# Attention, a gated network and a squared-clip network on one core: stores of the weight work, its allowances, and when k, v and streamed halves are asked for

## The chip, the cores and the metric

The kernel runs on 1 core of one Trainium2 chip. The metric is device time in microseconds (us), the median of several runs. Engines are written as in the profile: PE (TensorE, PEld its weight loads), DVE (VectorE), ACT (ScalarE), POOL (GpSimd) and SP (SyncE, which here issues all DMAs; SPq is its queue).

## What is computed

```python
kv = np.einsum('bhsd,bhse->bhde', k, v)              # 8 batches, 8 heads, 576 positions, 64
out = np.einsum('bhsd,bhde->bhse', q, kv)
rms = np.sqrt(np.mean(out * out, axis=-1, keepdims=True) + 1e-06)
x = (out / rms * g_norm)                             # then 4608 tokens x 512
x = (sigmoid(x @ w_gate) * (x @ w_val)) @ w_out      # 512 -> 1536 -> 512
h = x @ w_in                                         # 512 -> 2048
g = np.where(h >= 1, h, np.where(h <= -1, 0, (h + 1) ** 2 / 4))
return g @ w_out2                                    # 2048 -> 512
```

## The kernel before

Everything is float32. A product is made of three products of rounded halves (`mm3`, L86 to L90): high by high, high by low, low by high. `split` (L66) makes the two halves of an operand: ACT copies the high one (L69), DVE subtracts to get the low one (L77). The weights arrive as 64-bit words and are decoded on the chip.

The 4608 tokens are 9 blocks `j` of 512, and the 1536 hidden columns are 12 blocks `f`. Blocks 0 and 1 are done first, together. Blocks 2, 3 and 4 go one after the other, in 12 steps `f` each (loop from L1173): the sums for gate and value of `f + 1` (24 matmuls, `h`), sigmoid and product (`gf`, L553), the halves of that (`gh`, `gl`), then the 12 matmuls of `down(j, f)` into `acc`. Block 4 is called the tail. The attention and the normalisation of the next block run beside these steps (`norm_stage` in five stages, placed by `norm_plan` at points (f, 0), (f, 1), (f, 2)).

Blocks 5, 6 and 7, 8 are two pairs (`Pair`, loop from L1225). A pair computes gate and value of both blocks by seven products of half-size blocks (`pA` to `pE`, L631) in place of eight; it needs for that seven combinations of each weight block, which are read from DRAM (`w1d`). After the 12 steps of a pair come `down(j + 1, 0)`, `down(j, 11)`, and then the last down phase, `down(j + 1, f)` for f = 1 to 11, 12 matmuls each. The second network (`Second`) does the same trick with `w2d` and `wo2d`.

The weight work makes these combinations. It is one long list of single instructions (`weights_work`): for each `f` the stores of the halves of gate and value, two sums (`wsum`), four combinations (`su`), and their halves (`halves_out`, tiles `w2half`) with stores; then 24 units for the second network, each with a load (`raw`), a decode (one ACT, five DVE instructions, L463 to L473), combinations, halves and stores. Every entry is marked D (DVE), A (ACT) or S (a store). `work(dve, act)` (L1162) takes entries from the list until a kind is used up:

```python
left, begun = {"D": dve, "A": act, "S": 1}, False
while ahead[0] and left[ahead[0]] and not (begun and ahead[0] == "S"):
    left[ahead[0]] -= 1
    begun = True
    ahead[0] = next(todo, None)
```

so an S ends an allowance unless it comes first in it. Calls of `work` stand twice in each step of blocks 2 to 4 and three times in each step of a pair. What is left after the last pair's steps is done at once (`while ahead[0]: work(9, 9)`, L1274), ahead of `store(j)`, of the halves for the rest of the last down phase and of the x and weights of the second network (`second.begin()`).

All loads and stores stand in one order on SP. The halves of the down weights (`woh`) are streamed from DRAM by `stream_wo`; `stream(n)` asks for more until n are held.

Of the kernel before, what the change touches and what calls it, by code (L numbers as in the profile page):

```python
# [33 lines left out]
def attn_gated_mlp_kernel(ctx: ExitStack, tc: tile.TileContext, a: dict, out: bass.AP):  # L34
# [204 lines left out]
    def norm_plan(chunks, every):  # L239

        plan = {}
        for i, (j, p) in enumerate(chunks):
            f = every * i
            for n, place in enumerate(((f, 2), (f + 1, 0), (f + 1, 1), (f + 1, 2), (f + 2, 1))):
                plan.setdefault(place, []).append((j, p, n))
        for place in plan.values():
            place.sort(key=lambda x: -x[2])
        return plan
# [178 lines left out]
    OPS = ("a11", "a12", "a22", "s1", "s2", "s4", "s3")  # L427

    def w1_steps(f):

        gate, value = (wgv[f, i] for i in range(2))
        d = w1d[f]
        yield "S"
        store_halves(gate, [d[:, 0:2, h] for h in range(2)])
        store_halves([t[:, 2 * P:] for t in value], [d[:, 2, h] for h in range(2)])
        ts = []
# [54 lines left out]
    def halves_out(src, dst):  # L491

        n = src.shape[-1]
        halves = [half_tile(wop, "w2half", "wo")[:, :n] for _ in range(2)]
        yield "A"
        act_copy(halves[0], src)
        yield "D"
        nc.vector.tensor_tensor(out=halves[1], in0=src, in1=halves[0].bitcast(F32), op=ALU.subtract)
        yield "S"
        store_halves(halves, [dst(h) for h in range(2)])  # L500

# [81 lines left out]
    class Pair:  # L583
# [59 lines left out]
        def step(self, side, j, f, at, more):  # L643
# [13 lines left out]
            u2 = saved(A, "u2", "sig", 1)  # L657
            work(1, 1)
            D = bank(side, 2, "pD")
# [13 lines left out]
            at(3)  # L673
            work(2, 1)
            if f == F1 - 1:
# [259 lines left out]
    with tc.manual_schedule():  # L935
# [226 lines left out]
        def work(dve, act):  # L1162

            left, begun = {"D": dve, "A": act, "S": 1}, False
            while ahead[0] and left[ahead[0]] and not (begun and ahead[0] == "S"):
                left[ahead[0]] -= 1
                begun = True
                ahead[0] = next(todo, None)

        last = NB - 1  # L1170
        pair = Pair()
        chunks = lambda *js: [(j, p) for j in js for p in range(NP)]
        for j in range(2, J0):  # L1173
            tail = j == J0 - 1
# [6 lines left out]
            for f in range(F1):  # L1181
# [4 lines left out]
                if f + 1 < F1:  # L1186
                    g = gate_value(f + 1, xs)
                    split_g(j, f + 1, g)
                if not tail:
                    work(4, 2)  # L1190
                elif f < 9:
                    work(2, 1)
                at(f, 1)
                if j + 2 < B and f in ((2, 5) if tail else (3, 7)):
# [12 lines left out]
                if not tail:  # L1207
                    work(4, 2)
                elif f < 8:
# [8 lines left out]
                if tail and f == 9:  # L1218
                    pair.load(1)

        kv_done = J0 + 1
        pairs = range(J0, NB, 2)
# [6 lines left out]
        for k, j in enumerate(pairs):  # L1229
# [6 lines left out]
            if more:  # L1236
# [5 lines left out]
                for u in range(2):  # L1242
                    b = ((j + 3 + u) * T - 1) // S
                    if b > kv_done:
                        kv_done = b
                        for i in range(2):
                            plan.setdefault((4 * u + i, 2), []).insert(0, (kv_product, b, i))
                            for p in range(2 * i, 2 * i + 2):
                                plan.setdefault((4 * u + i - 1, 3), []).append((load_kv, b, p))
                        if u == 0:  # L1250
                            for p in range(2):
                                load_kv(b, p)

# [19 lines left out]
            else:  # L1273
                while ahead[0]:  # L1274
                    work(9, 9)
                store(j)
                early_end.close()
                second = Second()
                second.begin()
            for f in range(1, F1):  # L1280
                if f + 1 < F1:
                    split_g(j + 1, f + 1, pair.g2[f + 1])
                if more:
                    run(steps, 3)
                    if f in (3, 6):
                        pair.load(f // 3 - 1)
                else:
                    if f > 1:
# [52 lines left out]
```

## Time and profile before

| | us |
|---|---|
| median of 3 runs (1823.65 to 1828.53) | 1827.46 |
| the profiled execution | 1818.42 |
| its span | 1816.6 |
| PE busy (94%) | 1710.7 |
| DVE busy (60%) | 1081.4 |
| ACT busy (45%) | 816.1 |

The span of the trace lies within the profiled execution's own time. The share of busy time is an average over stages; where PE is idle, the list of its waits tells what ended each wait, and the tables by window tell what the other engines and the DMAs did in a stretch. PEclk is the granted clock of PE as a share of 2.4 GHz.

### The profile page before, as it was taken

To read this page: it belongs to the slowest core of one execution; us is meant where nothing else is said; L and a number is where in the kernel's file an instruction comes from. 1 tells how busy PE (TensorE), PEld (TensorE's weight loads), DVE (VectorE), ACT (ScalarE), POOL (GpSimd) and SP (SyncE) were. 2 spreads that over 40 slices of the span, in tenths; PEclk is the share of its full clock that TensorE was granted. 3 is DMA by queue.
4 is the path that set the end of the run, shared out by engine and by line. 5 is a ranking of instruction groups with operands and counts; after the bars stand their busy time and mean duration, and the time that the engine had idled before them with its cause. 6 is when DMAs were issued, how large, how long until landed. Compare 5 with 4: busy or idle time off the path is not lost.

```text
span 1816.6 us, 23149 instructions
## 1 busy us (share of the span) xinstructions
PE 1710.7 (94%) x8552; PEld 1444.6 (80%) x8552; DVE 1081.4 (60%) x1898; ACT 816.1 (45%) x1391; POOL 1.0 (0%) x8
## 2 busy tenths in 40 slices
PE   8999999999999899999990299999999999999999
PEld 5778787888877777788870189899899898998997
DVE  3788745464556567765666455655655556556553
ACT  3353445445376477643342244434444444444442
POOL 0000000000000000000000000000000000000000
PEclk7999999999999999999995599999999999999999
DMA  8554687566645767596755776344344343342430
GB/s 222 180 179 158 209 278 234 187 215 210 218 148 185 249 219 247 189 374 222 275 165 194 267 265 249 108 180 156 116 163 157 116 162 134 139 163 93 180 122 35
DMA packets 156832, 343.45 MB, mean 189 GB/s; under 512 B 15400, under 2 KB 64680, under 8 KB 150576
## 3 DMA queue, kind: packets, MB, share of 16 engines
q1 hardware_dynamic: 156720, 341.98, 55.5%
q8 instruction: 67, 1.10, 0.3%
q14 instruction: 45, 0.37, 0.1%
HBM read 264.85 MB, written 77.07 MB: 188 GB/s over the span
## 4 chain that ended last, share of the span: by engine, by line
PE 86%; DVE 7%; DMA 3%; ACT 2%; issue 1%; SPq 0%; DVEq 0%; ACTq 0%
PE acc L89 9%; PE acc L88 9%; PE acc L90 9%; PE h L88 6%; PE h L89 6%; PE h L90 6%; PE chB L775 6%; PE pA L631 5%; PE chA L775 4%; PE acc L775 4%; PE pE L631 3%; PE chC L775 3%; PE chD L775 3%; PE pC L631 2%; PE pD L631 2%; DMA raw<-in_w 1%
## 5 line engine op out<-in xcount | busy, mean ns | idle before, releaser
L88 PE MATMUL acc<-gh,woh 128*128 128x512 f32 x432 | 172.4, 399 | 80.7 <-ACT gh L69 71.1
L89 PE MATMUL acc<-gl,woh 128*128 128x512 f32 x432 | 171.2, 396 | 2.9 <-DVE gl L77 2.9
L88 PEld LDWEIGHTS acc<-gh,woh 128*128 128x128 f32 x432 | 82.1, 190 | 102.1 <-ACT gh L69 71.9
L88 PE MATMUL h<-xh,w 128*128 128x512 f32 x384 | 152.3, 397 | 0.0
L89 PE MATMUL h<-xl,w 128*128 128x512 f32 x384 | 150.4, 392 | 0.1
L90 PE MATMUL h<-xh,w 128*128 128x512 f32 x384 | 150.4, 392 | 0.0
L90 PE MATMUL acc<-gh,woh 128*128 128x512 f32 x336 | 132.7, 395 | 0.2 <-DMA woh<-wo1d 0.2
L90 PE MATMUL acc<-wo,gh 128*128 128x512 f32 x336 | 132.4, 394 | 0.0
L89 PE MATMUL acc<-wo,gh 128*128 128x512 f32 x336 | 132.2, 394 | 0.0
L88 PE MATMUL acc<-wo,gh 128*128 128x512 f32 x336 | 130.9, 390 | 0.0
L631 PE MATMUL pA<-xc,wc 128*128 128x512 f32 x432 | 110.8, 392 | 0.5 <-ACT s L69 0.5
L553 DVE TENSOR_TENSOR gf<-sig,h 128x512 f32<-128x512 f32 x60 | 41.2, 687 | 100.5 <-PE h L90 87.9
L89 PEld LDWEIGHTS acc<-gl,woh 128*128 128x128 f32 x432 | 82.2, 190 | 22.3 <-DVE gl L77 4.8
L69 ACT ACTIVATE gh<-g 128x384 fp32r<-128x384 f32 (+1 forms) x120 | 63.5, 541 | 76.4 <-PE acc L90 54.6
L631 PEld LDWEIGHTS pA<-xc,wc 128*128 128x128 f32 x432 | 81.3, 189 | 18.2 <-ACT s L69 1.0
L88 PEld LDWEIGHTS h<-xh,w 128*128 128x128 f32 x384 | 72.7, 189 | 20.1 <-issue 4.4
L704 DVE TENSOR_TENSOR gh<-c,gh 128x384 fp32r<-128x384 f32 x96 | 53.6, 558 | 57.3 <-ACT gh L69 56.6
L89 PEld LDWEIGHTS h<-xl,w 128*128 128x128 f32 x384 | 72.7, 189 | 15.1 <-DVE xl L77 0.4
L90 PEld LDWEIGHTS h<-xh,w 128*128 128x128 f32 x384 | 72.5, 189 | 15.2
L704 DVE TENSOR_TENSOR c<-chD,p 128x384 f32<-128x384 f32 x48 | 26.8, 558 | 92.1 <-ACT v L787 81.4
L90 PEld LDWEIGHTS acc<-gh,woh 128*128 128x128 f32 x336 | 64.2, 191 | 14.2 <-DMA woh<-wo1d 0.6
L704 DVE TENSOR_TENSOR g<-vp,g 128x768 f32<-128x768 f32 x48 | 46.0, 959 | 48.2 <-ACT vp L787 48.2
(222 smaller groups left out, 3807.0 us busy)
## 6 DMA issues: line engine op xcount, KB each, us to landing
wst<-w2d SPq DMA_DIRECT2D x48, 1792.0 KB, 7.4
woh<-wo1d SPq DMA_DIRECT2D x168, 256.0 KB, 5.0
wc<-w1d SPq DMA_DIRECT2D x168, 256.0 KB, 5.3
raw<-in_w SPq DMA_DIRECT2D x32, 512.0 KB, 4.9
raw<-in_w_gv SPq DMA_DIRECT2D x24, 512.0 KB, 4.3
w1d<-w2half SPq DMA_DIRECT2D x48, 256.0 KB, 2.2
w2d<-w2half SPq DMA_DIRECT2D x48, 256.0 KB, 2.8
kvraw<-in_kv_main SPq DMA_DIRECT2D x24, 448.0 KB, 5.3
```

What stands on the lines that cost most here:

```text
L69: nc.scalar.activation(out=o, in_=i, func=AF.Copy)
L88: nc.tensor.matmul(ps, w[0][:, wsl], x[0], start=first, stop=False)
L89: nc.tensor.matmul(ps, w[0][:, wsl], x[1], start=False, stop=False)
L90: nc.tensor.matmul(ps, w[1][:, wsl], x[0], start=False, stop=last)
L553: nc.vector.tensor_tensor(out=g, in0=sig, in1=value, op=ALU.mult)
L631: nc.tensor.matmul(o, w[:, h, sl], x[c][l], start=first and c == n == 0, stop=c == 1 and n == 2, skip_group_check=True)
L704: nc.vector.tensor_tensor(out=o, in0=x, in1=y, op=op)
L775: nc.tensor.matmul(bank[:, :T2], self.ws[w][h][:, sl], self.xo[x][:, l, c], start=first and c == n == 0, stop=c == 1 and n == 2, skip_grou ...
```

## The change

Stores of the weight work are put in a list `stores` and written out at the start of the next `work` call; they are no entries of the work list any more, so nothing but D and A ends an allowance. Allowances change: `work(5, 2)` for `work(4, 2)` at the end of a step of blocks 2 and 3; in a step of a pair `(1, 1), (1, 1), (3, 0)` in the first and `(2, 1), (3, 1), (3, 0)` in the second, for `(1, 1), (2, 1), (3, 0)` in both. In blocks 2 to 4 the norm stage at point 1 stands before the halves of `gf` and the weight work, not behind them, and `norm_plan` sorts the stages of a point the other way (stage 0 last). The k and v that the first pair needs are asked for in step 9 of the tail (`kv_ahead`), not at the pair's start. After the last pair's `store(j)`, `stream(6)` asks for halves before `second.begin()`.

```diff
@@ norm_plan
-            place.sort(key=lambda x: -x[2])
+            place.sort(key=lambda x: x[2] if x[2] else 9)
@@ w1_steps, halves_out
+    stores = []
...
-        yield "S"
-        store_halves(gate, [d[:, 0:2, h] for h in range(2)])
-        store_halves([t[:, 2 * P:] for t in value], [d[:, 2, h] for h in range(2)])
+        stores.append((gate, [d[:, 0:2, h] for h in range(2)]))
+        stores.append(([t[:, 2 * P:] for t in value], [d[:, 2, h] for h in range(2)]))
...
-        yield "S"
-        store_halves(halves, [dst(h) for h in range(2)])
+        stores.append((halves, [dst(h) for h in range(2)]))
@@ Pair.step
-            work(1, 1)
+            work(1, 1) if more else work(2, 1)
...
-            work(2, 1)
+            work(1, 1) if more else work(3, 1)
@@ work
-            left, begun = {"D": dve, "A": act, "S": 1}, False
-            while ahead[0] and left[ahead[0]] and not (begun and ahead[0] == "S"):
+            while stores:
+                store_halves(*stores.pop(0))
+            left = {"D": dve, "A": act}
+            while ahead[0] and left[ahead[0]]:
                 left[ahead[0]] -= 1
-                begun = True
                 ahead[0] = next(todo, None)
@@
+        kv_done = [J0 + 1]
+
+        def kv_ahead(j):
+
+            b = ((j + 3) * T - 1) // S
+            if j + 2 < NB and b > kv_done[0]:
+                for p in range(2):
+                    load_kv(b, p)
@@ blocks 2 to 4
                 if f + 1 < F1:
                     g = gate_value(f + 1, xs)
+                at(f, 1)
+                if f + 1 < F1:
                     split_g(j, f + 1, g)
                 if not tail:
                     work(4, 2)
                 elif f < 9:
                     work(2, 1)
-                at(f, 1)
...
                 if not tail:
-                    work(4, 2)
+                    work(5, 2)
...
                 if tail and f == 9:
                     pair.load(1)
+                    kv_ahead(J0)
@@ pairs
-                        if u == 0:
-                            for p in range(2):
-                                load_kv(b, p)
...
-                while ahead[0]:
+                while ahead[0] or stores:
                     work(9, 9)
                 store(j)
+                stream(6)
                 early_end.close()
                 second = Second()
                 second.begin()
...
+                    if f == 9:
+                        kv_ahead(j + 2)
```

What this moves is seen in the order of the instructions on three engines.

DVE in a step of block 2, before, from the product `gf` of one step to that of the next (`w2half`: a half of the weight work, `m` and `t`: the norm stages, `kvw`: a copy of a k v product):

```order
L553 TENSOR_TENSOR gf<-sig,h_2926 128x512
L77 TENSOR_TENSOR gl<-gf,gh 128x512
L498 TENSOR_TENSOR w2half<-su,w2half 128x512
L225 TENSOR_SCALAR m<-SS 128x512
L72 COPY kvw_187<-kvps 128x128
L230 TENSOR_TENSOR t<-t,m 128x512
L553 TENSOR_TENSOR gf<-sig,h_3020 128x512
```

and the like step of the changed kernel, to within a row of its next `gf`:

```order
L553 TENSOR_TENSOR gf<-sig,h_2963 128x512
L225 TENSOR_SCALAR m<-SS 128x512
L77 TENSOR_TENSOR gl<-gf,gh 128x512
L454 TENSOR_TENSOR su<-su,wsum 128x256
L454 TENSOR_TENSOR su<-wsum,su 128x256
L454 TENSOR_TENSOR su<-wsum 128x256
L499 TENSOR_TENSOR w2half<-su,w2half 128x512
L72 COPY kvw_187<-kvps 128x128
L230 TENSOR_TENSOR t<-t,m 128x512
L499 TENSOR_TENSOR w2half<-su,w2half 128x512
L441 TENSOR_TENSOR wsum<-w 128x512 x2
L454 TENSOR_TENSOR su<-wsum 128x256
```

One weight instruction stood there where eight and more stand now, and `m` has come ahead of `gl`.

ACT behind the last pair's steps, before (`raw`, `dt`: the decode; `ev`: the copies of `store(j)`; `gh<-g`: halves for the last down phase; `x_b<-xin`: the second network's x):

```order
L463 ACTIVATE dt<-raw 128x512
L69 ACTIVATE w2half<-dt 128x512
L463 ACTIVATE dt<-raw 128x512
L69 ACTIVATE w2half<-dt 128x512
L69 ACTIVATE ev<-acc_7732 128x512
L69 ACTIVATE ev<-acc_7734 128x512
L69 ACTIVATE gh<-g_7832 128x512
L69 ACTIVATE gh<-g_7937 128x512
L69 ACTIVATE x_b_9204<-xin 128x768
L69 ACTIVATE gh<-g_8046 128x512
```

and now, from the last product of the pair (`u<-pA`):

```order
L69 ACTIVATE u_9064<-pA 128x512
L69 ACTIVATE gh<-g_7920 128x512
L69 ACTIVATE gh<-u_9064 128x512
L69 ACTIVATE gh<-g_8014 128x512
L69 ACTIVATE ev<-acc_8023 128x512
L69 ACTIVATE ev<-acc_8025 128x512
L69 ACTIVATE gh<-g_8127 128x512
L69 ACTIVATE gh<-g_8236 128x512
L69 ACTIVATE x_b_9208<-xin 128x768
L69 ACTIVATE gh<-g_8348 128x512
```

No decode stands ahead of `ev` and `gh` any more; `x_b` still stands ahead of the halves of `down(j + 1, 4)`.

SP at the same place, before (`wo1d`: streamed halves in DRAM, `wst`: weights of the second network):

```order
L523 DMA wo2d_145<-w2half 128x512 x2
L580 DMA x2d_177<-ev 128x512 x4
L736 DMA xin<-x2d_170 128x2x256 x2
L736 DMA xin<-x2d_171 128x2x256
L736 DMA xin<-x2d_170 128x2x256 x2
L736 DMA xin<-x2d_171 128x2x256
L724 DMA wst<-w2d_98 128x3584
L529 DMA woh<-wo1d_0_112 128x512
```

and now:

```order
L580 DMA x2d_177<-ev 128x512 x4
L529 DMA woh<-wo1d_0_112 128x512
L529 DMA woh<-wo1d_1_113 128x512
L529 DMA woh<-wo1d_0_114 128x512
L529 DMA woh<-wo1d_1_115 128x512
L529 DMA woh<-wo1d_0_116 128x512
L529 DMA woh<-wo1d_1_117 128x512
L529 DMA woh<-wo1d_0_118 128x512
L529 DMA woh<-wo1d_1_119 128x512
L736 DMA xin<-x2d_170 128x2x256 x2
L736 DMA xin<-x2d_171 128x2x256
```

Eight loads of halves have come ahead of the loads of x and of the second network's weights.

## Rows read from the trace of the kernel before

**Rows 1.** The page, 40 equal slices of the span.

```profile
PE   8999999999999899999990299999999999999999
...
PEclk7999999999999999999995599999999999999999
```

**Rows 2.** Waits of PE, whole span: us in total, times, longest us.

```profile
PE acc L88 <- ACT gh L69: 71.1, 2, 70.1
PE acc L88 <- DMA woh<-wo1d: 9.6, 1, 9.6
```

**Rows 3.** Windows: us, then busy (x instructions) by engine, PEclk, DMA share, GB/s.

```profile
952.70:1022.80 70.10, 0.00 (x0) 0.00 (x0) 48.00 (x87) 18.61 (x33) 0.00 (x0) 0.54 0.57 190
1022.80:1043.40 20.60, 10.72 (x24) 7.60 (x25) 4.98 (x7) 2.68 (x4) 0.00 (x0) 0.59 1.00 361
```

**Rows 4.** Timeline of PE, last down phase: start us, us, instruction [idle before].

```profile
949.80 0.39 PE L88 MATMUL acc<-gh,woh 128*128 128x512 f32 x1
...
952.29 0.39 PE L90 MATMUL acc<-gh,woh 128*128 128x512 f32 x1
...
1022.81 0.79 PE L88 MATMUL acc<-gh,woh 128*128 128x512 f32 x1 [70.14 <-ACT gh L69]
...
1039.10 0.63 PE L89 MATMUL acc<-gl,woh 128*128 128x512 f32 x1
...
1042.51 0.63 PE L88 MATMUL acc<-gh,woh 128*128 128x512 f32 x1
...
1065.44 1.23 PE L775 MATMUL chA<-x_b,wst 128*128 128x384 f32 x6
```

**Rows 5.** Groups on DVE, 952.7 to 1022.8: xcount, busy us, mean ns, idle before.

```profile
L469 DVE SCALAR_TENSOR_TENSOR dt<-raw,dt 128x512 f32<-128x512 uint32 x11 | 7.6, 693 | 0.4
...
L498 DVE TENSOR_TENSOR w2half<-dt,w2half 128x512 fp32r<-128x512 f32 x9 | 6.2, 689 | 4.2 <-ACT w2half L69 4.2
...
L465 DVE TENSOR_SCALAR du<-dt 128x512 uint32<-128x512 uint32 x11 | 4.7, 424 | 17.5 <-ACT dt L463 17.5
```

**Rows 6.** Timeline of SP, last down phase.

```profile
1022.62 1.80 SPq L580 DMA_DIRECT2D x2d<-ev  x4
1024.52 3.47 SPq L736 DMA_DIRECT2D xin<-x2d  x6
1028.09 0.41 SPq L724 DMA_DIRECT2D wst<-w2d  x1
1028.60 15.74 SPq L529 DMA_DIRECT2D woh<-wo1d  x14
```

**Rows 7.** Timeline of ACT, last down phase.

```profile
1028.89 0.84 ACT L69 ACTIVATE x_b<-xin 128x768 fp32r<-128x768 f32 x1 [5.61 <-DMA xin<-x2d]
```

**Rows 8.** Windows, blocks 2 and 3.

```profile
267.80:371.80 104.00, 104.00 (x548) 84.59 (x547) 56.03 (x100) 48.06 (x74) 0.00 (x0) 1.00 0.64 204
371.80:477.30 105.50, 105.50 (x554) 85.85 (x553) 57.46 (x102) 48.29 (x75) 0.00 (x0) 1.00 0.67 212
```

**Rows 9.** Waits of DVE, 267.8 to 477.3 (blocks 2 and 3).

```profile
DVE gf L553 <- PE h L90: 66.0, 23, 5.5
DVE gl L77 <- ACT gh L69: 16.1, 23, 0.7
```

**Rows 10.** Waits of PE, 500 to 560 (block 4).

```profile
PE X L178 <- DVE m L225: 4.2, 3, 2.1
```

**Rows 11.** Waits of PE, 560 to 610 (into the first pair).

```profile
PE kvps L154 <- DMA kvraw<-in_kv_main: 3.9, 2, 2.1
```

**Rows 12.** Timeline of PE, first pair's first step.

```profile
600.52 1.52 PE L631 MATMUL pE<-xc,wc 128*128 128x512 f32 x6
604.15 0.33 PE L154 MATMUL kvps<-kvraw 112*64 112x64 f32 x2 [2.11 <-DMA kvraw<-in_kv_main]
...
608.46 2.27 PE L631 MATMUL pA<-xc,wc 128*128 128x512 f32 x6
```

**Rows 13.** DMA issues of the page: xcount, KB each, us to landing.

```profile
woh<-wo1d SPq DMA_DIRECT2D x168, 256.0 KB, 5.0
```

More of the change, by code (lines that the diff above doesn't have):

```diff
@@ L1219, in attn_gated_mlp_kernel @@
                     pair.load(1)
-        kv_done = J0 + 1
+                    kv_ahead(J0)
         pairs = range(J0, NB, 2)
@@ L1243, in attn_gated_mlp_kernel @@
                     b = ((j + 3 + u) * T - 1) // S
-                    if b > kv_done:
-                        kv_done = b
+                    if b > kv_done[0]:
+                        kv_done[0] = b
                         for i in range(2):
```

## The prediction

> **What bounds the kernel now.** I read the page's slices first. PE is busy nine tenths or more nearly everywhere, but two neighbouring slices past the middle show 0 and 2, with the granted clock at 5 tenths [rows 1]. Then the list of PE's waits, to see who ended them: one single wait of 70.1 us ended by ACT (`gh`), and one of 9.6 us ended by a load of streamed halves [rows 2]. The windows around them show what the others did: for 70.1 us PE does nothing while DVE is busy 48.0 us with 87 instructions, and in the 20.6 us after it PE has a mean clock of 0.59 and the DMAs a share of 1.00 at 361 GB/s [rows 3]. The groups on DVE in that stretch are the decode and the halves of the weight work [rows 5]. So the place is the drain of what the work list still holds after the last pair: `gh` for `down(j + 1, 2)` stands behind it on ACT. Everywhere else PE is the bound, with short waits before the first pair [rows 10, 11].
>
> The reader should see in the PE timeline how long the last down phase is [rows 4]: twelve matmuls of `down(j + 1, 1)` start from 949.80 to 952.29, 0.2264 us apart (2.49 over 11), so one `down` is 2.72 us. `down(j + 1, 2)` could start at 952.52; the second network starts at 1065.44. That is 112.9 us for ten downs worth 27.2 us, so **85.7 us** of this phase are not PE's work at full clock: 70.1 of drain, 9.6 of waiting for halves, and some 5 of slow matmuls (0.426 us apart from 1039.10 to 1042.51, eight intervals).
>
> **The change, part by part.**
>
> *The drain.* The work list, counted against the allowances as the code has them, holds 336 D and 104 A. Before, 84 S stand between them, and the steps of blocks 2, 3, 4 and of the two pairs take 48, 52, 30, 55 and 60 D; 91 D and 31 A are left. Without S in the list they take 108, 101, 31, 52 and 44 D, and the list is empty in step 8 of the last pair. The order on ACT says the same: no decode stands ahead of `ev` and `gh` there. So the 85.7 us go, less what the last down phase will wait for instead.
>
> *What is late next there.* Call T the end of `down(j, 11)` (949.8). The four stores of `ev` follow one after the other and take 1.8 us to issue [rows 6], so SP is free for the eight loads of `stream(6)` at about T + 1.5. The halves of `down(j + 1, 3)` land 5.0 us later [rows 13], T + 6.5, and are wanted at T + 5.4: a wait of 1.1. Eight issues at 0.45 us, then x: issued from T + 5.1. Before, the first x split began 4.4 us after the first x load was issued [rows 6, 7]. So ACT gets x at T + 9.5, works 0.84 us, and only then makes the halves of `down(j + 1, 4)`, whose `gl` follows the x subtraction on DVE: about T + 12 against T + 8.2. I take **4 us** for all waits of this phase together. Below, 0, if x lands before it is wanted. Above, 14.5, the 9.6 us and the 5 us of slow matmuls that before shows [rows 2, 4], since the same loads pass the same queue.
>
> *Blocks 2 and 3.* This is where the work goes: 209 D in place of 100. In these 209.5 us DVE is busy 113.5 us [rows 8]. A long D costs 0.69 us, a short one 0.42 [rows 5]; the eight D of a gate and value block are four of each (4.4 us), a unit of 18 D for the second network's first weights comes to 10.0, one of six to 3.6. What is added in the two blocks is four of the units of 18, six of those of six and five more D, less four that stood there: **62.6 us**. Free before: 66.0 us in which DVE waits for PE's sums before `gf`, and 16.1 us in which it waits for ACT's `gh` before `gl` [rows 9]; in 16 of the 24 steps the stage that now stands ahead of `gl` fills that 0.7 us, which gives 11 more. So 77 us are free for 62.6: it fits, but barely, and the steps differ by 2 us. Late `gf` costs nothing until PE wants its bank again, 5.4 us on (one `down` and one sum of 12 matmuls). I take **4 us** of PE waits. Below, 0. Above, 28: in the drain 85 weight instructions took 70.1 us, 0.82 each, against a busy mean of 0.56, and 109 more of them, each 0.26 us longer and nothing hidden, are 28. I stay near the lower end because the two windows show PE without a gap and DVE with a third of its time free [rows 8, 9]. The DMAs there: 5.5 more weight blocks of 1.84 MB (7 x 2 x 256 x 128 floats) in block 2 are 10.1 MB in 104 us, 97 GB/s on top of 204, which is under the 361 that the chip moved [rows 3]. ACT goes from 48 us to about 57 and 63 of some 105.
>
> *The pairs.* 52 D for 55 and 44 for 60: nothing gained or lost, PE is full there.
>
> *`at(f, 1)` ahead.* In block 4 the X products waited three times, 4.2 us, for `m`, which stood behind `gl` and two weight entries on DVE [rows 10]. It now follows `gf` at once, 2 us sooner, and the longest of these waits is 2.1: **4.2 us** gained (0 at worst). `gl` comes up to 2.2 us later in the tail and is wanted a whole step later: nothing.
>
> *k and v sooner.* PE waited 3.9 us for them in the first pair [rows 11], and the first six matmuls behind took 2.27 us where six take 1.52 [rows 12]: **4.6 us** gained. Their four loads now pass SP ahead of the last halves for the tail, which are asked for two steps before use. The next two k v loads still wait for the tile that the first product frees, as before.
>
> The other edits cost nothing: stores leave at the next call of `work`, where an S that did not come first also had to wait.
>
> **The sum** is -85.7 + 4 + 4 - 4.2 - 4.6 = **-86.5 us**. Against the profiled execution's 1818.4 this gives 1731.9. That execution is 9.0 us under the median of the runs, 1827.5; the same saving on the median gives **1741**. PE's own busy time, 1710.7 less the 5 of slow matmuls, stays below both.
>
> One row speaks of the clock: after the gap of about 4 us for k and v the next six matmuls cost 0.75 us more and those after nothing [rows 12], so short waits are dear by less than their length. The Trainium skill (TensorE: Matmul & The Clock Gate, section HAM oscillation) says that idle gaps between bursts of matmuls throw PE back to the halved clock, each time anew, and that this doubles what follows. By the row the new 4 us wait in the last down phase costs under 1 us more; by the rule it could bring back the 5 us of slow matmuls, 1746.
>
> **The rivals.**
>
> *DVE becomes the bound in blocks 2 and 3.* For: 62.6 us into 77, in order, with ACT and DVE waiting for each other at every half. Against: unused time is there in nearly every step. Price 5 to 28 us, with 16 in the middle: 1753 at 16, 1765 at 28.
>
> *The last down phase still starves.* For: 2.1 MB of halves now stand ahead of x, and x ahead of halves 4 on ACT. Against: four halves are ahead of need. At its bound, 14.5 in place of 4: 1752.
>
> *Slower than before: the clock falls in blocks 2 and 3.* If DVE's lateness opens a gap in every step, PE could run these steps at its lower level. A matmul is then 0.426 us from the next and not 0.226 [rows 4], 0.20 more, 7.2 us for the 36 matmuls of a step. Twelve of the 24 steps at that level (86 us) eat the whole gain, and all 24 (173 us) give 1914. For it: the clock was 0.59 behind the two long waits [rows 3]. Against: the gaps would be of one or two us, and block 4 has three of that kind with no such loss [rows 10]. The rule of the Trainium skill named above is the mechanism.
>
> *It does not do what it says.* If entries stayed over, a part of the hole would stay: half of it is 35 us, 1776. The order on ACT speaks against it.
>
> **How the numbers follow.** Forecast 0.75 (own range 1729 to 1751), DVE as the bound 0.14, starving 0.08, the clock 0.02, left-over work 0.01. The low end is all waits at 0 (1733) with the spread of the runs below it, 4 us: 1729. The high end takes in starving and DVE's case to its 28 us, 1765. A change of 0.3% (5.5 us) is about what a measurement of this kernel can tell from none. Only the clock case ends above; a hidden gain would take several cases at once: faster 0.97, same 0.01, slower 0.02.
>
> **What would show it.** PE's list of waits should have no ACT wait over 5 us, DVE should show 108 and 101 weight instructions in blocks 2 and 3 at 85% busy or more, and its wait for the sums should fall from 66.0 to under 15 us. The time from the end of `down(j, 11)` to the second network should be 34 us (115.6 before). The wait for X in block 4 and for k and v in the pair should be gone. I am wrong in the main if a wait of tens of us stays in the last down phase; wrong in size if PE shows more than 10 us of new waits in blocks 2 and 3, or if `gh` of `down(j + 1, 4)` comes later than T + 20.

## The result, and the profile after

The changed kernel takes 1754.09 us in the median of 4 runs (1749.44 to 1758.54); the kernel before took 1825.93 beside it (1823.65 to 1828.53). The ratio is 0.9606, with a 95% interval of 0.9574 to 0.9638. The predicted 1741 is 13 us too low; the range, 1729 to 1765, holds the result. The profiled execution took 1751.72 with a span of 1749.9, against 1816.6 before: 66.7 us less, where the sum gave 86.5.

The page's slices first (busy tenths of PE, granted clock of PE). The two slices of 0 and 2 are gone [rows 1].

```profile
PE   8999999999989999999999899999999999999999
...
PEclk7999999999999999999999999999999999999999
```

The timeline of PE gives marks for the stages: the first sums of block 2 and of block 4, the first `pA` of each pair, the last `pC` of the second pair, the first `chA` of the second network. Between them, in us:

| | before block 2 | blocks 2, 3 | block 4 | first pair | second pair's steps | last `pC` to second network | second network |
|---|---|---|---|---|---|---|---|
| before | 267.7 | 205.4 | 121.1 | 204.5 | 142.8 | 124.0 | 751.2 |
| after | 271.1 | 214.5 | 120.1 | 200.5 | 147.0 | 45.4 | 751.2 |
| difference | +3.4 | +9.1 | -1.0 | -4.0 | +4.2 | -78.6 | 0 |
| predicted | 0 | +4 | -4.2 | -4.6 | 0 | -81.7 | 0 |

So the hole was closed nearly as forecast. Of the 20 us by which the span missed the forecast, 3 are in the last phase, 13 in the four stages from block 2 to the second pair's steps, and 3.4 ahead of block 2. This last part is not the change's: the program up to there is the same, and over the 14 kernels of this study that stretch lies between 267.7 and 274.2 (the loads of `kv_early` come in earlier or later, and the mean granted clock there is 0.95 in the shortest and 0.93 in the longest).

PE's waits of the whole span (us in total, times, longest) name the places. The 71.1 us for `gh` [rows 2] are 5.0 now, X's wait for `m` [rows 10] is not in the list, `sig` is new, and `sqh`, `sql` and `s`, 0.5 to 0.6 us each before, have grown. The longest are:

```profile
PE h L88 <- ACT sig L550: 5.2, 1, 5.2
PE acc L88 <- ACT gh L69: 5.0, 1, 5.0
PE SS L223 <- ACT sqh L69: 4.7, 3, 2.0
PE kvps L154 <- DMA kv_early<-in_kv_main: 3.9, 2, 2.6
PE kvps L154 <- DMA kvraw<-in_kv_main: 3.3, 3, 1.7
PE pA L631 <- ACT s L69: 2.8, 2, 2.3
PE SS L223 <- DVE sql L77: 2.3, 5, 1.4
```

**Blocks 2 and 3.** Windows of block 2 and of block 3 (PE, PEld, DVE, ACT, POOL busy, granted clock, DMA share, GB/s), the successors of [rows 8]:

```profile
271.30:377.40 106.10, 103.86 (x543) 83.83 (x542) 80.26 (x147) 55.26 (x86) 0.00 (x0) 1.00 0.95 312
377.40:487.80 110.40, 105.91 (x548) 84.47 (x547) 86.74 (x152) 58.07 (x94) 0.00 (x0) 1.00 0.75 247
```

DVE is busy 76 and 79% of the time, not the 85% expected, and still PE waits. What stands still is the queues. DVE's waits there (the successors of [rows 9]), then ACT's, and last the one such wait of ACT in the kernel before:

```profile
DVE gf L553 <- PE h L90: 21.2, 11, 5.0
...
DVE gl L77 <- ACT gh L69: 4.9, 7, 0.7
```

```profile
ACT w2half L69 <- DVE su L454: 18.4, 15, 3.7
ACT w2half L69 <- DVE dt L474: 17.1, 8, 3.8
```

```profile
ACT w2half L69 <- DVE su L453: 18.7, 10, 2.5
```

DVE still waits 21.2 us for sums, in 11 of some 23 steps, so it has time left. ACT however stands 35.5 us (18.7 before) in front of `w2half` copies, waiting for DVE's weight instructions, with the split of `sq` of the next norm stage behind them on its queue. `SS` on PE wants that split. PE's waits for `SS` are 6.8 us of the 9.1 by which these blocks grew; 2.3 stand in no row of waits.

**The last down phase.** Windows (the same columns), then two rows of ACT and one of PE (start, us, the instruction, the idle time before it and its releaser):

```profile
971.00:974.00 3.00, 0.02 (x1) 0.02 (x1) 0.56 (x1) 1.36 (x2) 0.00 (x0) 0.71 1.10 350
974.00:977.00 3.00, 2.72 (x6) 1.83 (x7) 3.00 (x5) 2.10 (x3) 0.00 (x0) 0.50 1.12 445
977.00:980.00 3.00, 3.00 (x10) 2.37 (x9) 1.21 (x2) 0.18 (x1) 0.00 (x0) 0.65 0.94 375
```

```profile
972.57 0.84 ACT L69 ACTIVATE x_b<-xin 128x768 fp32r<-128x768 f32 x1 [8.64 <-DMA xin<-x2d]
973.31 0.61 ACT L69 ACTIVATE gh<-g 128x512 fp32r<-128x512 f32 x1
```

```profile
973.98 0.80 PE L88 MATMUL acc<-gh,woh 128*128 128x512 f32 x1 [4.96 <-ACT gh L69]
```

`down(j, 11)` ends at 960.38, the T of the prediction; the second network starts at 998.71, so T to there is 38.3 us (34 predicted, 115.6 before). The place is the one named: ACT waits 8.64 us for x and the halves of `down(j + 1, 4)` stand behind, at T + 12.9 where T + 12 was forecast. The wait is 5.0. Behind it, from 973.98 to 979.57, the starts of twelve matmuls take 5.59 us where 12 x 0.2264 = 2.72 are due; 0.3 of that is a wait for `gl`, and the other 2.6 us, slow matmuls, were in no term.

**Buffers.** The remaining two waits belong together. At the start of block 4, on ACT and on SP (a row of SP spans its issues and the waiting in between):

```profile
491.43 0.60 ACT L69 ACTIVATE ev<-acc 128x512 f32<-128x512 f32 x1 [1.44 <-DVE w2half L499]
495.48 0.60 ACT L69 ACTIVATE ev<-acc 128x512 f32<-128x512 f32 x1 [3.45 <-DMA x2d<-ev]
```

```profile
492.05 4.48 SPq L580 DMA_DIRECT2D x2d<-ev  x4
496.58 3.94 SPq L523 DMA_DIRECT2D w2d<-w2half  x6
```

The pool `wo` has 12 tiles, for streamed halves, `w2half` and `ev` alike. Six halves of the weight work are finished ahead of `ev`, and their stores are issued only by the next `work`, behind the four stores of `ev`. DVE copies the first and the third `ev`, ACT the second and the fourth (the two rows). So the third finds no tile until the first is stored, and `sig` of block 4 stands behind the fourth on ACT. The second pair's start is the same in small, with two stores held:

```profile
811.44 2.58 PE L631 MATMUL pA<-xc,wc 128*128 128x512 f32 x6 [2.31 <-ACT s L69]
```

```profile
806.94 4.43 SPq L580 DMA_DIRECT2D x2d<-ev  x4
...
812.92 0.94 SPq L523 DMA_DIRECT2D w2d<-w2half  x2
```

### The profile page after: what moved, and what is told of

Same layout as the page of the kernel before. It is cut to its first block, busy times and chain, and to the rows that moved or that the text cites. A ratio compares the mean times of both kernels' runs of the same rounds, so it can differ in the third digit from the quotient of the medians.

```text
span 1749.9 us, 23146 instructions
## 1 busy us (share of the span) xinstructions
PE 1713.4 (98%) x8552; PEld 1446.6 (83%) x8552; DVE 1078.8 (62%) x1898; ACT 815.6 (47%) x1391; POOL 1.0 (0%) x8
## 4 chain that ended last, share of the span: by engine, by line
PE 88%; DMA 5%; DVE 3%; ACT 3%; issue 1%; SPq 0%; DVEq 0%; ACTq 0%
PE acc L89 9%; PE acc L88 9%; PE acc L90 9%; PE chB L775 6%; PE h L88 5%; PE pA L631 5%; PE h L89 5%; PE h L90 5%; PE chA L775 4%; PE acc L775 4%; PE pE L631 3%; PE chC L775 3%; PE chD L775 3%; PE pD L631 2%; PE pC L631 2%; PE chC L90 1%
## 5 line engine op out<-in xcount | busy, mean ns | idle before, releaser
L89 PEld LDWEIGHTS acc<-gl,woh 128*128 128x128 f32 x432 | 81.7, 189 | 19.7 <-DVE gl L77 2.4
```

Of the source, the lines that this page charges most:

```text
L89: nc.tensor.matmul(ps, w[0][:, wsl], x[1], start=False, stop=False)
```

## The experiments

Each kernel is the changed one with the edit shown, but for `stores_only`, which starts from the kernel before. Each ratio is to runs of the kernel before made beside it, whose median lies between 1822.37 and 1825.93; so where two edited kernels differ by a few us, the stages of their profiles tell more than the medians. In a table at the end are the stages of all of them.

### What closed the hole: stores_end and stores_only

`stores_end` puts the S entries back and keeps every other edit:

```diff
...
-        stores.append((halves, [dst(h) for h in range(2)]))
+        yield "S"
+        store_halves(halves, [dst(h) for h in range(2)])
...
-            while ahead[0] and left[ahead[0]]:
+            while ahead[0] and left[ahead[0]] and not (begun and ahead[0] == "S"):
...
```

> The changed kernel with the S entries back in the work list, all its other edits kept (allowances 5, norm stage ahead, k and v, six halves first). Theory A, the S entries alone decide what is left over: by the code's count 102 D and 34 A are left after the last pair, so the hole comes back, about 102 x 0.82 = 84 us without matmuls in the last down phase; blocks 2 and 3 lose their new waits (8 us). Time about 1754 + 84 - 8 = 1830, 1815 to 1840. Theory B, the larger allowances do it: a hole under 20 us and a time under 1775.

Measured: 1812.14 us, ratio to before 0.9935 (0.9920 to 0.9951). Waits of PE, whole span:

```profile
PE acc L88 <- ACT gh L69: 86.0, 2, 80.5
```

The hole is there, 80.5 us long beside 5.5 of a second wait, as theory A had it to 4 us. The time is 18 us under what was expected, and under theory A's range: I had not reckoned that the small edits are worth more when the weight work is light. Blocks 2 and 3 take 205.4 as before; block 4 takes 109.9 where it took 121.1, the first pair 197.2 for 204.5.

`stores_only` is the other half, the list `stores` in the kernel before and no other edit.

> The kernel before with the S entries taken out of the list and nothing else (allowances 4, norm stage behind, k and v late, no six halves first). Theory A, this one edit carries nearly all: 1 D and 1 A are left over, the hole is gone; X in block 4 waits its 4 us again and k and v theirs, blocks 2 and 3 lose less than the 8 us of the changed kernel, the last down phase without the halves asked first waits up to 10 us for them. Time 1752 to 1768, near 1760. Theory B, the other edits matter as much: 1780 or more.

Measured: 1758.59 us, ratio 0.9643 (0.9629 to 0.9656). Theory A: this one edit takes 65.3 us off the kernel beside it, where the whole change took 71.8. The allowance at the end of a step is still 4 here and no hole is left, so the larger one was not needed for that; and blocks 2 and 3 take 211.5 us, less than the changed kernel's 214.5. X waits again for `m`, and the last down phase for halves, since these stand behind x on SP, as before the change:

```profile
PE acc L88 <- DMA woh<-wo1d: 9.9, 1, 9.9
PE X L178 <- DVE m L225: 6.0, 4, 2.3
```

### The last down phase: x_late, halves_sooner, x_first

`x_late` starts the x splits two steps later:

```diff
-                    if f > 1:
+                    if f > 3:
                         run(second.xsteps, 1)
```

> The changed kernel, whose last down phase starts the x splits of the second network two steps later (f > 3 for f > 1). Theory A, the 5.0 us wait of PE for gh and the slow matmuls behind it come from the x split that waits for its load on ACT ahead of gh: the wait goes to under 1 us and the stretch from the last pC to the second network falls from 45.4 to 37 to 39 us. Time 1746 to 1749. Theory B, the loads bind: PE then waits as long for woh or for x_b at the second network, the stretch stays within 2 us of 45 and the time at 1754.

Measured: 1756.53 us (0.9631, 0.9618 to 0.9644), no gain. PE's waits from the last `pC` on:

```profile
PE acc L88 <- DMA woh<-wo1d: 3.9, 1, 3.9
PE chA L775 <- ACT u L69: 2.7, 1, 2.7
```

The wait for `gh` is gone and one for `woh` has come, 8 us later; the stretch is 43.9 for 45.4, and the second network loses 4.5 because its last x splits come late. Theory B: with the gap behind ACT closed, the loads end the same phase.

`halves_sooner` asks for six halves from step 10 of the last pair on:

```diff
-                stream(2 if f < 8 else 4)
+                stream(2 if f < 8 else 4 if more or f < 10 else 6)
...
-            stream(4)
+            stream(4 if more else 6)
             down(j + 1, 0)
```

> The changed kernel, which in the last pair asks for six halves ahead from step 10 on, and again behind the steps, in place of four, so that x stands right behind the stores of ev on SP. Theory A, the last down phase waits because of the order of the loads (eight halves ahead of x, when no DMA ran just before): the 5.0 us wait for gh goes under 1 us, no wait for woh takes its place, the stretch from the last pC to the second network falls from 45.4 to 37 to 39 us, time 1746 to 1748. Theory B, the bytes bind (the DMAs are at 350 to 390 GB/s there whatever the order): a wait of 3 us or more for woh or wst comes later, the stretch stays at 43 or more, time 1752 or more.

Measured: 1752.00 us (0.9600, 0.9577 to 0.9622). The edit did less than its expectation says: the two downs ahead of the store free two pairs of tiles, so four loads of halves still stand ahead of x on SP.

```profile
966.35 2.05 SPq L529 DMA_DIRECT2D woh<-wo1d  x4
968.45 3.21 SPq L736 DMA_DIRECT2D xin<-x2d  x6
```

The wait for `gh` falls to 2.2 us and the stretch to 42.1, between the two theories. `x_first` therefore has the same `stream` calls and moves x ahead of these four:

```diff
-                stream(6)
                 early_end.close()
                 second = Second()
-                second.begin()
+                x = second.x_load(0)
+                stream(6)
+                second.begin(x)
```

> As halves_sooner, and x is asked for ahead of the last four loads of halves, the first weights of the second network behind them. Theory A, the last down phase waits for the order of its loads alone, and halves_sooner only moved x up by 2 us: x lands 4 us or more sooner than in the changed kernel, the waits for gh and woh together are under 1 us, the stretch from the last pC to the second network is 37 to 39 us (45.4 in the changed kernel, 42.1 in halves_sooner), time 1745 to 1748. Theory B, the bytes bind: a wait of 3 us or more for woh or wst takes its place and the stretch stays at 42 or more, time 1750 or more.

Measured: 1749.91 us (0.9580, 0.9561 to 0.9599). x is split 6.8 us sooner behind the end of `down(j, 11)` and the wait for `gh` is gone, as expected. But the stretch is still 42.1, with this wait, which ends at 985.00, and the DMAs at a share of 0.96 to 1.10 in the 9 us around its start:

```profile
PE acc L88 <- DMA woh<-wo1d: 2.6, 1, 2.6
```

```profile
975.00:978.00 3.00, 2.91 (x12) 1.95 (x12) 2.75 (x4) 2.08 (x4) 0.00 (x0) 1.00 1.10 444
978.00:981.00 3.00, 3.00 (x15) 2.48 (x14) 2.09 (x4) 1.37 (x2) 0.00 (x0) 1.00 0.96 399
981.00:984.00 3.00, 1.39 (x7) 0.81 (x5) 2.09 (x4) 1.47 (x3) 0.00 (x0) 1.00 1.03 380
```

By its bounds this is theory B, if barely (42.1 for 42, 2.6 for 3). The order of the loads is worth 3.3 us of the changed kernel's loss. That the bytes are the rest is not shown: `all` and `all_four_held` below have the same loads in the same order behind the stores of `ev`, wait at most 0.6 us for `woh` there, and have stretches of 40.1 and 39.1.

### The held buffers: stores_first and f11_light

`stores_first` issues pending stores (`put_stores`, the loop that `work` begins with) at two more places:

```diff
                 if f == F1 - 1:
+                    put_stores()
                     store(j, None)
...
             acc_side[0] = side
+            put_stores()
             stream(4)
```

> The changed kernel, which issues the pending stores of the weight work before the ev copies of a block and behind a pair's steps, not at the next allowance only. Theory A, stores that wait for the next allowance hold w2half tiles that ev needs: the 5.2 us wait of PE for sig at the start of block 4 falls to under 2.5, the 2.3 us wait for s at the second pair's start to under 0.5, the slow matmuls there go too. Time 1746 to 1750. Theory B, ACT and DVE are simply behind with their work there: both waits stay within 1 us of 5.2 and 2.3, time 1754.

Measured: 1749.61 us (0.9594, 0.9582 to 0.9607). At the second pair theory A is right: the steps take 142.8 us, as before the change, and the 4.2 us are gone. At block 4 it is wrong, the wait is 5.4. SP shows why: the six stores now go first, but the halves themselves are finished just ahead of `ev`, and the third `ev` (DVE) waits for their stores in place of those of `ev`.

```profile
492.83 4.37 SPq L523 DMA_DIRECT2D w2d<-w2half  x6
497.29 2.87 SPq L580 DMA_DIRECT2D x2d<-ev  x4
```

```profile
497.27 0.69 DVE L72 COPY ev<-acc 128x512 f32<-128x512 f32 x1 [2.95 <-DMA w2d<-w2half]
```

`f11_light` takes that allowance away:

```diff
-                if not tail:
+                if not tail and f < F1 - 1:
                     work(4, 2)
+                elif not tail:
+                    work(0, 0)
```

> The changed kernel without the allowance ahead of down(j, 11) in blocks 2 and 3 (pending stores are issued there, nothing is computed). Theory A, the six w2half tiles of that allowance hold the buffers and stand ahead of ev on ACT and DVE: the 5.2 us wait for sig at the start of block 4 falls under 1 us, the list is empty in step 10 of the last pair in place of 8, time 1749 to 1750. Theory B, the wait comes with the copies and stores of ev alone, whatever stands ahead: it stays at 4 us or more, time 1754.

Measured: 1744.39 us (0.9562, 0.9539 to 0.9585), 9.7 under the changed kernel. There is no wait of PE from 480 to 510 us, and block 4 takes 111.1 for 120.1. So it was the finished halves that stood ahead of `ev`, in buffers and on the queues (theory A); 9 us and not 5, in part because the clock fell behind that wait (below). Blocks 2 and 3 lose 3.7 us of it: other entries of the list fall on the steps of block 3, PE has a new wait of 2.0 us for `sig` there, and the granted clock fell to 0.50 behind that wait and behind one for `SS`. The second pair's steps take 142.8 here too: other entries of the list fall on its start.

### Blocks 2 and 3: split_early, norm_behind, old_sort

`split_early` moves one copy on ACT and one subtraction on DVE ahead of the allowance of 5:

```diff
-            for n, place in enumerate(((f, 2), (f + 1, 0), (f + 1, 1), (f + 1, 2), (f + 2, 1))):
+            for n, place in enumerate(((f, 2), (f, 2), (f + 1, 1), (f + 1, 2), (f + 2, 1))):
...
-            place.sort(key=lambda x: x[2] if x[2] else 9)
+            place.sort(key=lambda x: x[2] if x[2] > 1 else 8 + x[2])
```

> The changed kernel, whose norm stage 1 (the split of sq) stands at point (f, 2) behind stage 0, ahead of the allowance of 5, in place of point (f + 1, 0) behind it. Theory A, the new waits of blocks 2 and 3 are SS waiting for sqh and sql, which stand behind the weight work: SS's 7.0 us fall under 1.5, time 1747 to 1749. Theory B, DVE's and ACT's density is the bound there: the time lost goes over to other waits (gh, sig, X) and the two blocks keep their 8 us, time 1754.

Measured: 1745.22 us (0.9571, 0.9548 to 0.9594). PE's waits in blocks 2 and 3 are one line, and the two blocks take 207.1 us for 214.5, with the same PEld work (166.9 us) and DVE nearly as busy (164.0 us here, 165.0 in the changed kernel). Theory A: it was the order, not DVE's density.

```profile
PE h L88 <- ACT sig L550: 0.7, 1, 0.7
```

`norm_behind` puts `at(f, 1)` back behind the halves of `gf` and the weight work, with the new sort kept:

```diff
-                at(f, 1)
                 if f + 1 < F1:
                     split_g(j, f + 1, g)
                 if not tail:
                     work(4, 2)
                 elif f < 9:
                     work(2, 1)
+                at(f, 1)
```

> The changed kernel with the norm stage at point 1 back behind the halves of gf and the weight work. Theory A, the move gained what X waited for in block 4: PE waits there 4 to 6 us for m again, blocks 2 and 3 are as they are, time 1757 to 1760. Theory B, the move is what makes SS wait in blocks 2 and 3 (it brings SS's stage forward): the waits of SS fall under 3 us, and the time is 1754 or less.

Measured: 1771.19 us (0.9709, 0.9684 to 0.9734), 17 us over the changed kernel. Both theories fall. X does not wait for `m` in block 4 (0.2 us); the loss is in blocks 2 and 3, 226.9 us for 214.5: 6 us more of waits for `SS`, and slow matmuls, since behind three of these waits, of 2.7 to 3.5 us, the granted clock was 0.50. PE's waits of the whole span, DVE's in the two blocks and ACT's in the two blocks:

```profile
PE SS L223 <- ACT sqh L69: 6.7, 3, 3.1
PE SS L223 <- DVE sql L77: 6.2, 6, 3.5
```

```profile
DVE gl L77 <- ACT gh L69: 16.8, 24, 0.7
```

```profile
ACT r L228 <- DVE m L225: 11.7, 7, 2.6
```

`m` now stands behind `gl` and four weight entries, ACT waits 11.7 us for it, and 24 waits of up to 0.7 us ahead of `gl` are back (16.8 us, 16.1 in [rows 9], 4.9 in the changed kernel). That is the 11 us of DVE's time that the prediction gave to the moved stage. `stores_end` shows that the move is worth nothing in these blocks where the weight work is light: 205.4 us with it, 205.4 before it. And `stores_only`, with the stage behind, takes 211.5; it differs in the allowance of 4 and in the old sort, and no run tells which of the two makes the move matter.

`old_sort` undoes the other half:

```diff
-            place.sort(key=lambda x: x[2] if x[2] else 9)
+            place.sort(key=lambda x: -x[2])
```

> The changed kernel with norm_plan's old order of the stages of one point (stage 4 ahead of 2), the norm stage still ahead of the weight work. Theory A, it was the order of the stages that took X's wait for m in block 4 away (norm_behind kept it away without the move): X waits 3 to 6 us for m again, time 1757 to 1760. Theory B, either edit is enough: X waits under 1 us and the time is 1754.

Measured: 1754.13 us (0.9609, 0.9592 to 0.9625), the time of the changed kernel; X does not wait for `m` in block 4. Theory B: the moved stage and the new sort each take that wait away, and only with both undone (`stores_only`) it is back.

### Together: all and all_four_held

`all` has `stores_first`, `f11_light`, `split_early` and `x_first`.

> The changed kernel with four edits together: pending stores ahead of ev and behind a pair's steps, no allowance ahead of down(j, 11) in blocks 2 and 3, sq's split at point (f, 2), x first in the last down phase. Theory A, the four losses are in four places and add up: SS 7, sig and s 5 + 4, last down phase 7, in all 23 us under the changed kernel's 1754: 1726 to 1738. Theory B, they are one loss of DVE's that moves on when a place is mended: 1741 or more, with new waits of PE of 8 us or more.

Measured: 1732.18 us (0.9488, 0.9473 to 0.9504). Theory A, the losses add up. One place got worse: the second pair's steps take 148.8 us. With `f11_light` the list ends in step 10, and `x_first` asks for six halves from that step on. SP then stands 13 us in loads that find no tile, ahead of the stores that would free one, and ACT and PE wait behind:

```profile
908.07 13.04 SPq L529 DMA_DIRECT2D woh<-wo1d  x4
921.20 0.86 SPq L523 DMA_DIRECT2D wo2d<-w2half  x2
```

```profile
926.22 0.63 ACT L69 ACTIVATE w2half<-dt 128x512 fp32r<-128x512 f32 x1 [7.74 <-DMA wo2d<-w2half]
```

```profile
927.39 2.92 PE L631 MATMUL pA<-xc,wc 128*128 128x512 f32 x6 [2.80 <-ACT s L69]
```

`all_four_held` keeps four in the steps:

```diff
-                stream(2 if f < 8 else 4 if more or f < 10 else 6)
+                stream(2 if f < 8 else 4)
```

> As all, but the steps of the last pair hold four halves to their end, and six are asked for only behind the steps, after the pending stores. Theory A, the second pair's steps took 148.8 us in all (142.8 in stores_first and f11_light) because loads of halves without a free buffer stood on SP ahead of the last stores of the weight work, in step 10 and 11: the steps go back to 143, PE's wait of 2.8 us for s and the 6 us go, time 1724 to 1729. Theory B, they are slower because the list now ends two steps later, whatever SP does: the 148 us stay and the time stays at 1732 or more.

Measured: 1731.34 us (0.9497, 0.9481 to 0.9514). In the stage theory A is right: 142.8 us again, no wait of 2.8. In the time it is not: the median is 2 us above the upper end and no better than that of `all`, since in its profile blocks 2 and 3, the same code, take 210.5 us for 206.9. There too a store came late. On ACT the same `w2half` copy of block 3, in `all` and in `all_four_held`:

```profile
396.71 0.63 ACT L69 ACTIVATE w2half<-su 128x512 fp32r<-128x512 f32 x1 [0.66 <-DMA w2d<-w2half]
```

```profile
397.90 0.63 ACT L69 ACTIVATE w2half<-su 128x512 fp32r<-128x512 f32 x1 [2.72 <-DMA w2d<-w2half]
```

`sig` stands behind it, PE waits 2.96 us for that in place of 0.91, and the granted clock fell behind the longer wait alone. Either version beats both kernels, by about 22 us against the changed one.

| us | before block 2 | blocks 2, 3 | block 4 | first pair | second pair's steps | last `pC` to second network | second network |
|---|---|---|---|---|---|---|---|
| stores_end | 274.1 | 205.4 | 109.9 | 197.2 | 144.4 | 129.5 | 751.2 |
| stores_only | 274.2 | 211.5 | 123.0 | 204.1 | 142.8 | 50.1 | 751.2 |
| x_late | 273.3 | 214.5 | 120.0 | 200.8 | 147.0 | 43.9 | 755.7 |
| halves_sooner | 273.9 | 215.9 | 120.4 | 200.9 | 146.8 | 42.1 | 751.2 |
| x_first | 273.8 | 214.5 | 120.1 | 202.5 | 147.4 | 42.1 | 751.2 |
| stores_first | 269.0 | 218.9 | 121.1 | 200.1 | 142.8 | 44.8 | 751.2 |
| f11_light | 273.3 | 218.2 | 111.1 | 199.7 | 142.8 | 45.6 | 751.2 |
| split_early | 271.0 | 207.1 | 120.0 | 201.7 | 145.7 | 45.3 | 751.2 |
| norm_behind | 274.2 | 226.9 | 122.8 | 201.8 | 146.8 | 45.2 | 751.2 |
| old_sort | 270.9 | 216.0 | 120.4 | 201.8 | 145.2 | 45.8 | 751.3 |
| all | 273.5 | 206.9 | 111.1 | 198.3 | 148.8 | 40.1 | 751.3 |
| all_four_held | 272.6 | 210.5 | 111.1 | 199.7 | 142.8 | 39.1 | 751.2 |

## Why the prediction was right, and where its sizes were off

**The drain.** Right, in mechanism and count: in the trace DVE has 240 weight instructions by the end of block 4, as counted (108 + 101 + 31), and none behind the last `pC`, and with the S entries back (`stores_end`) the hole is 80.5 us. The page's two empty slices, the one wait in PE's list and the DVE groups in that window were enough to see it.

**"I take 4 us for all waits of this phase together."** The place, the cause and the time of `gh` (T + 12.9) were as worked out; the phase lost 38.3 - 29.9 = 8.4 us, within the bound of 14.5. What was mis-sized: 2.6 us of slow matmuls behind the wait, which no term had, 1.3 us more of waits (5.3 with one for `gl`), and 0.5 that no row names.

**"I take 4 us of PE waits" in blocks 2 and 3.** The waits were 6.8 us and the stage grew by 9.1, inside the range of 0 to 28, but for another reason than either end. I compared DVE's added work with DVE's free time and asked when a late `gf` would hurt. DVE did keep up. The late thing was `sqh`, an ACT copy for the norm that stood behind the added `w2half` copies, and PE reaches `SS` in the middle of the step. The expected mark, DVE at 85% with waits for sums under 15 us, was missed (76 and 79%, 21.2 us), and `split_early` takes 7.4 of the 9.1 back by moving one copy and one subtraction.

**X in block 4, -4.2.** The wait went, as said; either of two edits takes it. It was worth more: `stores_end` shows block 4 at 109.9, 11.2 us under before. 6.4 of these are waits, X's 4.2 among them, and 4.8 are PE's busy time (114.7 to 109.9). The prediction took block 4 as three short gaps "with no such loss" of the clock [rows 10], and that was misread. Behind the longest of them, 2.07 us up to 551.74, the kernel before shows

```profile
552.00:555.00 3.00, 3.00 (x17) 1.70 (x14) 1.92 (x3) 2.23 (x5) 0.00 (x0) 0.50 0.01 3
```

The changed kernel keeps only 1.0 of the 11.2.

**"The other edits cost nothing: stores leave at the next call of `work`."** This sentence failed. It looked at when the stores are issued and not at what they hold. Finished halves keep their tiles of the pool `wo`, and `ev` takes four of that pool at the end of a block. That is 10 us at the start of block 4 (120.1 against 109.9; `f11_light` gets 9.0 back by finishing none there) and the 4.2 us of the second pair (`stores_first` gets all of it), which I had put at nothing. It is also why PE's list has an ACT wait over 5 us, which the prediction had ruled out.

**k and v, -4.6.** The first pair gained 4.0, but that the size fits is luck. The 3.9 us at the first product [rows 11] are gone, and the second product, whose loads are issued only behind the first, now waits as it did not before. PE's list of waits in the pair has

```profile
PE kvps L154 <- DMA kvraw<-in_kv_main: 2.9, 2, 1.7
```

so k and v gave 1.0 us of waits, and the clock falls behind them as before. Of the rest, 2.2 us are waits for `gl` (1.2) and for `m` (1.0), which the changed kernel no longer has in this pair and `stores_only` still has. The smaller allowance in the pair may be what took them away; no run isolates it, nor the early loads.

**The rivals.** Density of DVE, starving and the falling clock did not come as priced. The forecast's own range ended at 1751, and the measured 1754 lies above it; the whole range holds it by the room left for DVE's case, which came in another way, and that is luck in part. Starving has a part of 4.4 us, of which order is 3.3 (`x_first`). The clock's case has a small footing: in the changed kernel's profile blocks 2 and 3 show a granted clock of 1.00 throughout, but in that of `halves_sooner` the same wait for `SS` is followed by 0.50, and the two blocks take 215.9 us for 214.5; in that of `stores_first` this came twice, and they take 218.9. Single gaps do it there, not every step, so it is far from the 86 us of that case.

**The clock.** The prediction set a row, under 1 us, against a rule of the Trainium skill, 5 us. The windows above show the granted clock at 0.71 in the wait of 5.0 us and at 0.50 and 0.65 behind it; the cost was 2.6 us, about in the middle. (The Trainium skill, TensorE: Matmul & The Clock Gate, section HAM oscillation, has idle gaps send the clock back each time; this trace agrees for the gaps of 5.0 and 5.2 us, and the 5 us that the prediction took from the rule were too many.) Two other gaps do the same. Behind the `sig` wait at block 4, and behind the 2.3 us at the second pair:

```profile
497.00:500.00 3.00, 3.00 (x8) 2.33 (x8) 2.23 (x5) 1.21 (x2) 0.00 (x0) 0.50 1.02 349
```

```profile
812.00:815.00 3.00, 3.00 (x8) 2.32 (x8) 0.00 (x0) 0.94 (x2) 0.00 (x0) 0.50 0.87 229
```

From 496.62 to 501.61 the starts of twelve matmuls take 4.99 us where 2.72 are due, and from 811.44 to 815.65 those of eleven take 4.21 for 2.49: 2.3 and 1.7 us more. 0.50 is the 1.2 GHz level. A gap of 2.0 us did so in some profiles and not in others. The longest wait for `SS` in block 2 is 2.01 us in the changed kernel and 2.00 in `halves_sooner`; the 3 us from 1.0 us behind it are, in this order:

```profile
342.60:345.60 3.00, 3.00 (x48) 2.52 (x48) 2.99 (x6) 2.64 (x4) 0.00 (x0) 1.00 0.98 322
```

```profile
345.45:348.45 3.00, 3.00 (x42) 2.72 (x42) 2.99 (x6) 2.64 (x4) 0.00 (x0) 0.52 0.96 315
```

**Still open.** Why the same gap of 2.0 us is followed by the lower clock level in one profile and not in the next. Also why `x_first` waits 2.6 us for its halves and `all_four_held` 0.6, with the same order of loads behind the stores of `ev`, and which of the small edits shortens the first pair.

## What to carry to other kernels

When work is spread into steps that have time left, compare it not with the free time of its engine alone: list what stands behind each added instruction on every in-order queue, and who wants that next. Then ask what each added step holds until its store has landed; a shared pool runs out at the places where something else takes several tiles at once. A gap of more than 2 us on PE was mostly dearer here than its length, so a wait of a few us that is left is worth one more edit.

## What was not expected of the hardware

Gaps of 2.3, 5.0 and 5.2 us on PE were each followed by matmuls at the lower clock level and cost 1.7 to 2.6 us beyond their length. A gap of 2.0 us in block 2, with the same instructions around it, left the granted clock at 1.00 in one profile and was followed by 0.52 over 3 us in another, so the length of a gap does not settle its price. And the DMAs ran near their full share, 0.95, over the whole of block 2 at 312 GB/s without a wait for a load in PE's list.
